# Casting loads for two batches of v, a PSUM bank per pair of heads, and a new order of steps in a linear-attention and FFN kernel

## The chip, the cores and the metric

The kernel runs on one core of a Trainium2 chip. The metric is the device time of one execution in microseconds; the time before is the median of three runs. A core has a matrix engine (TensorE, PE in the profile; its weight loads are PEld), VectorE (DVE), ScalarE (ACT), GpSimd (POOL) and SyncE (SP). They run side by side, each through its own list of instructions in order, and wait for each other by semaphores. GpSimd and SP mostly issue DMA transfers here.

## The reference

Linear attention over 8 batches, 8 heads, 576 positions and head size 64, then a multiplicative feed-forward network over the 4608 rows of 512:

```python
phi(x) = where(x > 0, x, exp(x) - 1) + 1          # = min(max(x, 0) + 1, exp(x))
kv  = sum over s of phi(k)[s, d] * v[s, e];  z = sum over s of phi(k)[s, d]
x   = (phi(q) @ kv) / (phi(q) @ z + 1e-6)
out = ((x @ w1) * (x @ w2)) @ w3 @ w_out
```

Inputs and output are float32.

## The kernel before, in words

Of the 576 positions of a batch, 512 are worked as 4 groups of 128 (`NJ`), the other 64 (`R`) of two batches together as one tile of 128 rows. Eight heads make four pairs (`KC`); a pair fills 128 partitions. The product w3 @ w_out is formed once on the chip (steps `w3t`, `w3c`, `wa`, `wf`, `wc`: w3 is transposed on TensorE, multiplied with w_out, and copied into `wf_sb`), so that each chunk of 512 rows needs only the two products of width 1024, their elementwise product and one more product.

A batch passes through these steps:

- `ld`, `lr`, `lp` load k, q and v; `x` (exp on ACT), `t` (max and add on DVE) and `m` (minimum on DVE) make phi; `xr`, `tr`, `mr` do so for the 64-row rest.
- `v` (L217) casts v to bf16 into `vt`, whose rows have 65 columns: 64 of v and a one, so that a single matmul yields kv and z.
- `kv` (batches 0 and 1) or `kk` (the others) multiply phi(k) with v into PSUM; `kc`, `kh`, `kg` copy the diagonal blocks into `kvb`, which memsets (`const` 4 to 11) have set to zero.
- `qt` and `qc` transpose phi(q) on TensorE for batches 0 and 1, `qd` by a DMA for the others. `na` multiplies with `kvb`; `nd` divides on DVE (add, reciprocal, multiply); `xp` and `xc` (batches 0 to 2) or `xd` (DMA) transpose the result into `xt`.
- Per chunk c and eighth f: step `f` makes both products (8 matmuls of 512 columns, 128 rows of w1 and w2 each), `ac` copies the one to SBUF on ACT, `ab` multiplies them on DVE; `o` makes 128 rows of the output (8 matmuls), `oc` copies them, `st` stores them. Chunk 8 holds the 64-row rests. `ol:7,3` is the last unit, made in two halves of 256 columns, one copied by DVE and stored by SP, one copied and stored by ACT.

PSUM has two pools: `mm_ps`, four tiles of one bank, and `at_ps`, two tiles of two banks, for kv, na and the first part of w3 @ w_out. In SBUF the load pool has 5 buffers, `o_sb` 5, phi of k and q one each, `ab` and `xt` 3.

The order is written out by hand: the string `ORDER` (from L478) lists single steps, and each engine gets its instructions in the order of that list. `v:1,6,2,a` is step `v` of batch 1, two heads from head 6, on ACT; a last letter v, a, g or s names VectorE, ScalarE, GpSimd or SP. `warm` steps are matmuls on zeros whose result nobody reads. `GATES` (L550) adds waits: a load given first may start only when the one given behind `<` has landed. The casting loads of weights (`l3`, `lo`, `lw`) and those of batches 0 and 1 stand in GpSimd's queue, one behind the other; each also waits until the eighth load before it has landed. Loads of later batches, the 64-row rests and DMA transposes stand in SP's queue.

Of the kernel before, what the change touches and what calls it, by code (L numbers as in the profile page):

```python
# [8 lines left out]
F32 = mybir.dt.float32  # L9
# [9 lines left out]
def kernel(  # L19
# [44 lines left out]
    ident = consts.tile([P, P], BF16)  # L64
    zero = consts.tile([P, NCH], BF16)
    vts = [wpool.tile([P, NJ, H, E1], BF16, name=f"vt{i}") for i in range(1)]
    vrz = wpool.tile([P, 2, H, E1], BF16)
    kvb = [wpool.tile([P, KC, 2, E1], BF16, name=f"kvb{i}") for i in range(B)]
# [22 lines left out]


    @step
    def const(i):
        if i == 0:
            nc.vector.memset(zero, 0.0)  # L96
        elif i == 1:
            make_identity(nc, ident)
        elif i == 2:
            for t in vts:  # L100
                nc.vector.memset(t[:, :, :, D:E1], 1.0)
        elif i == 3:
            nc.vector.memset(vrz, 0.0)
            for s in range(2):
                nc.vector.memset(vrz[s * R:(s + 1) * R, s, :, D:E1], 1.0)
        else:
            nc.vector.memset(kvb[i - 4], 0.0)
# [9 lines left out]
    def ld_(n, b, h0, nh, queue):  # L117
# [3 lines left out]
            in_=src[n][b, h0:h0 + nh, 0:NJ * P, :].rearrange("h (p j) d -> p h (j d)", j=NJ))  # L121

# [53 lines left out]
    @step  # L176
    def m(n, b, h0, hp):
        d = got(ph, (n, b), phi_p, [P, KC, NJ, 2, D], BF16, n)
        s = slice((2 * hp - h0) * W, (2 * hp - h0 + 2) * W)
        nc.vector.tensor_tensor(  # L180
            out=d[:, hp].rearrange("p j u d -> p u j d"),
            in0=ts[n, b, h0][:, s].rearrange("p (u j d) -> p u j d", u=2, j=NJ),
            in1=es[n, b, h0][:, s].rearrange("p (u j d) -> p u j d", u=2, j=NJ), op=ALU.min)
# [31 lines left out]
    @step  # L215
    def v_(b, h0, nh, eng):
        copy_of[eng](  # L217
            out=vts[b % len(vts)][:, :, h0:h0 + nh, 0:D],
            in_=raw["v", b].rearrange("p (h j d) -> p j h d", h=H, j=NJ)[:, :, h0:h0 + nh])

    @step
    def vr(b, eng):
        s = b % 2
        r = slice(s * R, (s + 1) * R)
        copy_of[eng](out=vrz[r, s, :, 0:D],
                     in_=raw["vr", b // 2][r].rearrange("p (h d) -> p h d", d=D))
# [3 lines left out]
    def kv(b, hp):  # L230
        o = got(ps, ("kv", b), at_ps, [P, 2, 512], F32, "at", "kvp")
        g, a = divmod(hp, 2)
        kj = ph["k", b]
        kr = ph["kr", b // 2, 2 if b > 1 else b]
        vt = vts[b % len(vts)]
        dst = o[:, g, a * PW:(a + 1) * PW]
        for j in range(NJ):
            nc.tensor.matmul(dst, kj[:, hp, j].rearrange("p u d -> p (u d)"),
                             vt[:, j, 2 * hp:2 * hp + 2, :].rearrange("p h e -> p (h e)"),
                             start=(j == 0), stop=False)  # L240
        nc.tensor.matmul(dst, kr[:, hp * P:(hp + 1) * P],
                         vrz[:, b % 2, 2 * hp:2 * hp + 2, :].rearrange("p h e -> p (h e)"),
                         start=False, stop=True)
# [4 lines left out]
    def kk(b, hp):  # L248
        o = got(ps, ("kk", b), at_ps, [P, 2, 512], F32, "at", "kvp")[:, 0]
        kj, kr, vt = ph["k", b], ph["kr", b // 2, 2], vts[b % len(vts)]  # L250
        for j in range(NJ + 1):
            for u in range(2):
                h = 2 * hp + u
                nc.tensor.matmul(o[u * D:(u + 1) * D, hp * E1:(hp + 1) * E1],  # L254
                                 kj[:, hp, j, u] if j < NJ else kr[:, h * D:(h + 1) * D],
                                 vt[:, j, h] if j < NJ else vrz[:, b % 2, h],
                                 start=(j == 0), stop=(j == NJ))

    @step
    def kg(b, r, eng):  # L260
        rows = slice(r * D, (r + 1) * D)
        copy_of[eng](out=kvb[b][rows, :, r, :], in_=ps["kk", b][rows, 0, 0:KC * E1].rearrange(
# [3 lines left out]
    def kc(b, g0, ng, r, eng):  # L266
        rows = slice(r * D, (r + 1) * D)
        copy_of[eng](  # L268
            out=kvb[b][rows, 2 * g0:2 * (g0 + ng), r, :].rearrange(
                "p (g a) e -> p g a e", a=2),  # L270
            in_=ps["kv", b][rows, g0:g0 + ng, 0:2 * PW].rearrange(
                "p g (a u e) -> p g a u e", a=2, u=2)[:, :, :, r, :])

    @step
    def kh(b, hp, r, eng):
        rows = slice(r * D, (r + 1) * D)
        g, a = divmod(hp, 2)
        c = a * PW + r * E1
        copy_of[eng](out=kvb[b][rows, hp, r, :], in_=ps["kv", b][rows, g, c:c + E1])

    @step
    def qt(b, h, n):
        t = ps["qt", b, h] = mm_ps.tile([P, NCH], F32, tag="mm", name="qtp").bitcast(
            BF16).rearrange("p (i t) -> p i t", t=P)
        for i in range(n):
            for j in range(NJ):
                nc.tensor.transpose(
                    t[:, i * NJ + j, :], ph["q", b][:, h + i, j].rearrange("p u d -> p (u d)"), ident)

    @step  # L290
    def qc(b, h, n, eng):
        d = got(sb, ("qt", b), att, [P, KC, NJ * P], BF16, "qt")
        copy_of[eng](out=d[:, h:h + n, :].rearrange("p i (j t) -> p (i j) t", t=P),
                     in_=ps["qt", b, h][:, 0:n * NJ, :])

    @step
    def qd(b):
        d = got(sb, ("qt", b), att, [P, KC, NJ * P], BF16, "qt")
        nc.sync.dma_start(out=d.rearrange("p c (j t) -> p (c j) t", t=P),
                          in_=ph["q", b].rearrange("p c j u d -> p (c j u d)"), transpose=True)  # L300
# [7 lines left out]
    def na(b, hp):  # L308
        o = ps["na", b, hp] = at_ps.tile([P, 2, 512], F32, tag="at", name="nd")
        for j in range(NJ):  # L310
            nc.tensor.matmul(o[:, j // 2, (j % 2) * 256:(j % 2) * 256 + PW],  # L311
                             sb["qt", b][:, hp, j * P:(j + 1) * P],
                             kvb[b][:, hp].rearrange("p u e -> p (u e)"),
                             start=True, stop=True)

    def divide(o, r, dst):
        nc.vector.tensor_scalar_add(out=r, in0=o[:, :, :, D], scalar1=1e-6)
        nc.vector.reciprocal(out=r, in_=r)  # L318
        nc.vector.tensor_tensor(  # L319
            out=dst, in0=o[:, :, :, 0:D],  # L320
# [269 lines left out]
```

## Time and profile before

| | us |
|---|---|
| runs before, median (lowest to highest) | 251.57 (251.06 to 251.97) |
| the profiled execution's own time | 251.52 |
| its span, first to last instruction | 249.7 |
| busy: TensorE / VectorE / ScalarE / GpSimd | 236.0 / 164.1 / 122.9 / 36.4 |
| first free run of FFN matmuls (`f`) from | 36.36 |
| first output unit (`o:0,0`) from | 55.30 |
| last matmul starts | 246.0 |

The span is what the engines' instructions cover; the time has some 1.8 us more around it. The page gives busy times per engine, the span in 40 slices, the DMA queues, the chain of work that ended last, and groups of instructions with their mean duration and what ended the idle time before them. The timeline, from which single lines are shown below, has: start, duration, engine, line, operation, tiles written and read, count, and in brackets the idle time before it and what ended that.

### The profile page before, as it was taken

To read this page: it belongs to the slowest core of one execution; us is meant where nothing else is said; L and a number is where in the kernel's file an instruction comes from. 1 tells how busy PE (TensorE), PEld (TensorE's weight loads), DVE (VectorE), ACT (ScalarE), POOL (GpSimd) and SP (SyncE) were. 2 spreads that over 40 slices of the span, in tenths; PEclk is the share of its full clock that TensorE was granted. 3 is DMA by queue.
4 is the path that set the end of the run, shared out by engine and by line. 5 is a ranking of instruction groups with operands and counts; after the bars stand their busy time and mean duration, and the time that the engine had idled before them with its cause. 6 is when DMAs were issued, how large, how long until landed. Compare 5 with 4: busy or idle time off the path is not lost.

```text
span 249.7 us, 4327 instructions
## 1 busy us (share of the span) xinstructions
PE 236.0 (95%) x1620; PEld 122.9 (49%) x1636; DVE 164.1 (66%) x364; ACT 122.9 (49%) x190; POOL 36.4 (15%) x59
## 2 busy tenths in 40 slices
PE   6897889979999989999999999999999999999994
PEld 6654844445444555454444454544544444444442
DVE  7518764977868999959649889786775365042320
ACT  3409554776956774665744835153352332323211
POOL 8554720001100210011000032200001100000000
PEclk9999999999999999999999999999999999999999
DMA  6999999999998999999999699975409511210155
GB/s 120 204 265 348 214 198 294 314 248 319 336 240 227 281 294 287 211 248 351 189 265 335 182 248 260 291 175 107 105 12 128 179 22 21 91 38 29 55 144 153
DMA packets 69621, 50.10 MB, mean 201 GB/s; under 512 B 41312, under 2 KB 64096, under 8 KB 69600
## 3 DMA queue, kind: packets, MB, share of 16 engines
q1 hardware_dynamic: 60416, 31.86, 54.1%
q0 software_dynamic: 9040, 17.83, 28.0%
q8 instruction: 13, 0.21, 0.3%
q10 hardware_dynamic: 144, 0.13, 0.2%
q14 instruction: 8, 0.07, 0.1%
HBM read 38.80 MB, written 9.44 MB: 193 GB/s over the span
## 4 chain that ended last, share of the span: by engine, by line
PE 56%; DMA 32%; DVE 4%; issue 3%; ACT 2%; POOL 1%; SPq 0%; ACTq 0%; POOLq 0%; DVEq 0%
PE a_ps L420 17%; PE o_ps L445 17%; PE b_ps L420 17%; DMA v<-in_v_dram 13%; DMA q<-in_q_dram 9%; DMA w_sb<-in_moe_w_dram 4%; DMA wo<-in_moe_w_out_dram 3%; DMA k<-in_k_dram 3%; DVE xn L319 2%; PE nd L311 2%; PE kvp L254 1%; POOL w3b L159 1%; PE ndr L336 1%; PE o_ps L472 1%; ACT vt L217 1%
## 5 line engine op out<-in xcount | busy, mean ns | idle before, releaser
L420 PEld LDWEIGHTS <-w_sb 128*128 128x128 bf16 x576 | 55.6, 98 | 64.6 <-issue 0.6
L439 DVE TENSOR_TENSOR ab<-a_sb,b_ps 128x512 bf16<-128x512 f32 x72 | 49.0, 684 | 43.7 <-PE b_ps L420 40.1
L434 ACT COPY a_sb<-a_ps 128x512 f32<-128x512 f32 x72 | 42.1, 584 | 58.8 <-PE a_ps L420 52.7
L420 PE MATMUL a_ps<-xt,w_sb 128*128 128x512 bf16 x256 | 66.0, 379 | 0.5 <-ACT xt L358 0.5
L420 PE MATMUL b_ps<-xt,w_sb 128*128 128x512 bf16 x256 | 66.0, 379 | 0.0
L445 PE MATMUL o_ps<-wf_sb,ab 128*128 128x512 bf16 x267 | 62.9, 379 | 1.0 <-issue 0.2
L445 PEld LDWEIGHTS <-ab 128*128 128x128 bf16 x280 | 26.4, 98 | 30.3 <-DVE ab L439 1.2
L463 POOL DMA_DIRECT2D out_dram<-o_sb x24 | 14.5, 605 | 148.7 <-ACT o_sb L451 130.9
L451 ACT COPY o_sb<-o_ps 128x512 f32<-128x512 f32 x24 | 14.0, 585 | 34.1 <-PE o_ps L445 31.9
L319 DVE TENSOR_TENSOR xn<-nd,r 128x512 bf16<-128x512 f32 x32 | 22.1, 692 | 1.1
L166 ACT ACTIVATE e<-q 128x1024 bf16<-128x1024 f32 x16 | 16.5, 1056 | 1.8 <-DMA q<-in_q_dram 1.8
L166 ACT ACTIVATE e<-k 128x1024 bf16<-128x1024 f32 x16 | 16.4, 1058 | 0.9 <-DMA k<-in_k_dram 0.8
L451 DVE COPY o_sb<-o_ps 128x512 f32<-128x512 f32 x11 | 7.6, 687 | 8.0 <-PE o_ps L445 8.0
L217 ACT CAST vt<-v 128x1024 bf16<-128x1024 f32 (+1 forms) x11 | 10.2, 933 | 5.4 <-PE kvp L254 2.7
L180 DVE TENSOR_TENSOR k<-t,e 128x512 bf16<-128x512 bf16 x32 | 12.2, 418 | 0.4 <-ACT e L166 0.2
L172 DVE TENSOR_SCALAR t<-q 128x1024 bf16<-128x1024 f32 x16 | 10.9, 688 | 2.1 <-DMA q<-in_q_dram 2.1
L180 DVE TENSOR_TENSOR q<-t,e 128x512 bf16<-128x512 bf16 x32 | 11.9, 420 | 0.2
L311 PE MATMUL nd<-kvb,qt 128*128 128x130 bf16 x128 | 10.9, 220 | 0.9 <-DVE kvb L268 0.4
L172 DVE TENSOR_SCALAR t<-k 128x1024 bf16<-128x1024 f32 x16 | 10.5, 688 | 1.2 <-DMA k<-in_k_dram 1.1
L311 PEld LDWEIGHTS <-qt 128*128 128x128 bf16 x128 | 8.7, 98 | 4.9 <-DVE xn L319 1.0
L113 PE MATMUL warm<-zero 128*128 128x128 bf16 x116 | 9.2, 241 | 1.2 <-DVE zero L96 1.2
L318 DVE RECIPROCAL r<-r 128x8 f32<-128x8 f32 (+1 forms) x40 | 8.1, 202 | 1.4
(76 smaller groups left out, 191.6 us busy)
## 6 DMA issues: line engine op xcount, KB each, us to landing
v<-in_v_dram SPq DMA_DIRECT2D x6, 1024.0 KB, 9.8
k<-in_k_dram SPq DMA_DIRECT2D x6, 1024.0 KB, 8.7
q<-in_q_dram SPq DMA_DIRECT2D x6, 1024.0 KB, 9.2
out_dram<-o_sb POOLq DMA_DIRECT2D x24, 256.0 KB, 6.1
w3b<-in_moe_w_dram POOLq DMA_DIRECT2D x8, 256.0 KB, 8.1
out_dram<-o_sb SPq DMA_DIRECT2D x7, 256.0 KB, 2.3
v<-in_v_dram POOLq DMA_DIRECT2D x3, 512.0 KB, 18.9
out_dram<-o_sb SPq DMA_DIRECT2D x9, 128.0 KB, 2.4
```

The source lines that it names most:

```text
L166: return nc.scalar.activation(out=e[:, 0:nh * W], in_=raw[n, b][:, h0 * W:(h0 + nh) * W], func=AF.Exp)
L172: nc.vector.tensor_scalar(out=d[:, 0:nh * W], in0=raw[n, b][:, h0 * W:(h0 + nh) * W], scalar1=0.0, scalar2=1.0, op0=ALU.max, op1=ALU.add)
L180: nc.vector.tensor_tensor(out=d[:, hp].rearrange("p j u d -> p u j d"), in0=ts[n, b, h0][:, s].rearrange("p (u j d) -> p u j d", u=2, j=NJ ...
L217: copy_of[eng](out=vts[b % len(vts)][:, :, h0:h0 + nh, 0:D], in_=raw["v", b].rearrange("p (h j d) -> p j h d", h=H, j=NJ)[:, :, h0:h0 + nh])
L311: nc.tensor.matmul(o[:, j // 2, (j % 2) * 256:(j % 2) * 256 + PW], sb["qt", b][:, hp, j * P:(j + 1) * P], kvb[b][:, hp].rearrange("p u e - ...
L319: nc.vector.tensor_tensor(out=dst, in0=o[:, :, :, 0:D], in1=r.unsqueeze(3).to_broadcast(list(r.shape) + [D]), op=ALU.mult)
L420: nc.tensor.matmul(o, w[:, kc, f * P:(f + 1) * P], xt_of(c)[:, :, kc, :], start=(kc == 0), stop=(kc == KC - 1))
L434: return copy_of[eng](out=d, in_=ps["a", c, f])
L439: nc.vector.tensor_mul(out=d[:, f, :], in0=sb["a", c, f], in1=ps["b", c, f])
L445: nc.tensor.matmul(d, sb["ab", c][:, f, m * P:(m + 1) * P], wf_sb[:, f, :], start=(f == 0), stop=(f == FC - 1))
L451: return copy_of[eng](out=d, in_=ps["o", c, m])
L463: queue_of[queue].dma_start(out=dst, in_=sb["o", c, m][r])
```

## The change

It has five parts.

1. `v` of batches 0 and 1 is loaded by GpSimd as bf16 (`lv`), without the step `v`; its tile has no ones. In `kv` a 128-column matmul on v is followed by one of two columns on a small tile of ones, with the same weights.
2. `vt`, `vrz` and `kvb` get a new layout: a pair of heads is one row of 130, a one at either end and 128 columns of v between. The cast `v` of later batches takes every second head (`u`) at once.
3. In `kv` each pair has a PSUM bank of its own: the four pairs of a batch take both `at_ps` tiles, where they shared one.
4. phi of k and q is laid out by group, then head; `m` takes the minimum over four heads in one instruction instead of two. `kk` is one step for all pairs of a batch.
5. `ORDER` is new nearly throughout; `st:8,3,s` stands behind `ol:7,3`. Functions `kz`, `nt`, `ln`, `xm` are added that no step of the list calls; a memset for their tile is called.

```diff
+    ones = consts.tile([P, 2], BF16)
+    eps = consts.tile([P, 1], F32)
...
+    kvz = wpool.tile([P, KC, P], BF16)
-    kvb = [wpool.tile([P, KC, 2, E1], BF16, name=f"kvb{i}") for i in range(B)]
+    kvb = [wpool.tile([P, KC, PW], BF16, name=f"kvb{i}") for i in range(B)]
...
+    def of_pairs(t):
+        return t.rearrange("p j (c u) e -> p j c (u e)", u=2)
+
+    def set_ones(t):
+        for c in (0, PW - 1):
+            nc.vector.memset(of_pairs(t)[:, :, :, c:c + 1], 1.0)
...
+        elif i == 12:
+            nc.vector.memset(ones, 1.0)
+            nc.vector.memset(eps, 1e-6)
+            nc.vector.memset(kvz, 0.0)
...
+    def lv(b, h0, nh):
+        if ("vb", b) not in raw:
+            raw["vb", b] = ld.tile([P, H * W], F32, tag="ld", name="vb").bitcast(
+                BF16)[:, 0:H * W].rearrange("p (h j d) -> p h j d", h=H, j=NJ)
+        return nc.gpsimd.dma_start(
+            out=raw["vb", b][:, h0:h0 + nh].rearrange("p h j d -> p h (j d)"),
+            in_=v[b, h0:h0 + nh, 0:NJ * P, :].rearrange("h (p j) d -> p h (j d)", j=NJ))
...
-    def m(n, b, h0, hp):
-        d = got(ph, (n, b), phi_p, [P, KC, NJ, 2, D], BF16, n)
-        s = slice((2 * hp - h0) * W, (2 * hp - h0 + 2) * W)
+    def m(n, b, h0, nh):
+        d = got(ph, (n, b), phi_p, [P, NJ, H, D], BF16, n)
         nc.vector.tensor_tensor(
-            out=d[:, hp].rearrange("p j u d -> p u j d"),
-            in0=ts[n, b, h0][:, s].rearrange("p (u j d) -> p u j d", u=2, j=NJ),
-            in1=es[n, b, h0][:, s].rearrange("p (u j d) -> p u j d", u=2, j=NJ), op=ALU.min)
+            out=d[:, :, h0:h0 + nh].rearrange("p j h d -> p h j d"),
+            in0=ts[n, b, h0][:, 0:nh * W].rearrange("p (h j d) -> p h j d", h=nh, j=NJ),
+            in1=es[n, b, h0][:, 0:nh * W].rearrange("p (h j d) -> p h j d", h=nh, j=NJ), op=ALU.min)
...
     def kv(b, hp):
-        o = got(ps, ("kv", b), at_ps, [P, 2, 512], F32, "at", "kvp")
         g, a = divmod(hp, 2)
-        dst = o[:, g, a * PW:(a + 1) * PW]
+        dst = got(ps, ("kv", b, g), at_ps, [P, 2, 512], F32, "at", "kvp")[:, a, 0:PW]
+        kj, kr, vb = ph["k", b], ph["kr", b // 2, b], raw["vb", b]
         for j in range(NJ):
-            nc.tensor.matmul(dst, kj[:, hp, j].rearrange("p u d -> p (u d)"),
-                             vt[:, j, 2 * hp:2 * hp + 2, :].rearrange("p h e -> p (h e)"),
-                             start=(j == 0), stop=False)
+            k2 = of_pair(kj[:, j], hp)
+            nc.tensor.matmul(dst[:, 1:PW - 1].rearrange("p (u d) -> p u d", u=2), k2,
+                             vb[:, 2 * hp:2 * hp + 2, j], start=(j == 0),
+                             stop=False, skip_group_check=True)
+            nc.tensor.matmul(dst[:, 0:PW:PW - 1], k2, ones, start=False, stop=False, skip_group_check=True)
```

The start and the end of the new list, and its stretch around the loads of batches 1 and 2:

```diff
+    const:0 const:5 lr:k,0,s l3:0 warm:26,0 const:1 warm:18,9 const:3 xr:k,0,0 lr:v,0,s tr:k,0,0 w3t:0
+    l3:1 l3:2 warm:8,1 zr:0,1 w3t:1 w3c:0,a l3:3 lo:0,2 lo:2,2 lo:4,2 lo:6,2 const:4 warm:8,2 l3:4 l3:5
+    const:12 w3t:2 w3c:1,a warm:8,3 ld:k,0,0,4,g w3t:3 w3c:2,v w3c:3,v warm:8,4 mr:k,0,0 wa:0,1
+    ld:k,0,4,4,g wa:1,1 wa:2,1 wa:3,1 wa:4,1 const:6 t:k,0,0,4 ld:q,0,0,4,g w3t:4 vr:0,a ld:q,0,4,4,g
+    wa:5,1 w3c:4,a wa:6,1 const:8 w3t:5 wf:4 x:k,0,0,4 wa:7,1 w3c:5,a lv:0,0,4 wc:4,v m:k,0,0,4 wc:2,a
+    warm:10,10 lv:0,4,2 wc:1,a lv:0,6,2 wc:3,a warm:10,11 warm:10,12 x:k,0,4,4 zr:0,0 t:k,0,4,4 wc:0,v
+    l3:6 warm:10,13 l3:7 lw:0,0,256 lw:1,0,256 x:q,0,4,4 t:q,0,0,4 lw:0,1,256 wf:5 kv:0,0 lw:1,1,256
+    lw:0,1,512 kv:0,1 m:k,0,4,4 t:q,0,4,4 const:2 m:q,0,4,4 x:q,0,0,4 qt:0,2,2 kv:0,3 kh:0,3,1,a
+    m:q,0,0,4 wc:5,a qt:0,0,2 kv:0,2 kh:0,3,0,v qc:0,2,2,v lw:1,1,512 kc:0,0,0,a kc:0,0,1,v w3t:6
+    kh:0,2,0,a na:0,3 qc:0,0,2,a kh:0,2,1,v ld:k,1,0,8,g nd:0,3 w3t:7 na:0,0 w3c:6,a na:0,2 xp:0,3
+    w3c:7,v xc:0,3,a nd:0,0 wf:6 nd:0,2 na:0,1 nd:0,1 xp:0,0 xp:0,2 wf:7 wc:6,v xp:0,1 xc:0,0,a xc:0,1,a
+    ld:q,1,0,8,g xc:0,2,v wc:7,v f:0,2 f:0,1 lr:k,1,s ac:0,2,a ac:0,1,a ab:0,2 lr:v,1,s fk:0,0,0,2
...
+    t:k,1,4,4 m:k,1,4,4 vr:1,v mr:k,0,1 x:q,1,4,4 f:0,5 t:q,1,4,4 kv:1,1 ld:k,2,0,8,s ld:v,2,0,8,s
+    ac:0,5,a ab:0,6 kv:1,0 kv:1,3 m:q,1,4,4 kv:1,2 kc:1,0,0,a kh:1,3,1,v t:q,1,0,4 kh:1,3,0,v qt:1,2,2
+    m:q,1,0,4 qc:1,2,2,a f:0,3 ac:0,3,a ab:0,5 qt:1,0,2 ab:0,3 kh:1,2,0,a kh:1,2,1,a kc:1,0,1,a na:1,3
+    na:1,2 nd:1,3 qc:1,0,2,a o:0,2 nd:1,2 xp:1,3 const:10 x:k,2,4,4 na:1,1 xc:1,3,v na:1,0 o:0,0
...
+    ab:8,5 o:8,1 o:8,2 o:8,0 oc:7,0,a oc:8,1,v o:8,3 oc:8,2,v oc:8,3,v oc:8,0,a st:7,0,s st:8,2,s
+    st:8,1,s st:8,0,s ol:7,3 st:8,3,s
```

The corresponding end of the list before was `... o:8,2 oc:8,0,v st:8,0,s o:7,0 oc:8,2,v st:8,2,s oc:7,0,a st:7,0,s ol:7,3`.

## The prediction

> **What bounds the kernel now.** I read the page first (busy time, the slices), then the sums by stage, then the chain, and last the timeline where the chain changes hands. One matmul can be reported busy while it only drains, so the page's 95% for TensorE is checked by the starts of the matmuls.
>
> ```profile
> PE 236.0 (95%) x1620; PEld 122.9 (49%) x1636; DVE 164.1 (66%) x364; ACT 122.9 (49%) x190; POOL 36.4 (15%) x59
> ...
> DMA  6999999999998999999999699975409511210155
> ```
>
> ```profile
> 0.00:36.00 36.00, 30.05 (x305) 21.40 (x309) 22.08 (x52) 17.38 (x26) 21.84 (x35) 1.00 1.09 226
> 36.00:63.00 27.00, 24.77 (x160) 13.05 (x162) 19.03 (x44) 18.01 (x30) 1.11 (x2) 1.00 1.09 291
> 63.00:125.00 62.00, 60.43 (x466) 30.05 (x470) 52.25 (x120) 41.14 (x63) 5.93 (x10) 1.00 1.10 265
> ...
> 190.00:249.70 59.70, 56.11 (x278) 26.59 (x278) 19.12 (x36) 17.37 (x30) 2.17 (x4) 1.00 0.33 86
> ```
>
> The columns are length, busy time of TensorE, weight load, VectorE, ScalarE and GpSimd, granted clock, DMA share, GB/s. The clock is full throughout. In the trace a 512-column matmul starts 0.216 us after the one before it (four of them make the chain's pieces of 0.86 us), a 128- or 130-column one 0.056 to 0.057 us. Where two starts lie further apart, TensorE lost the difference. Summed: 2.5 us until 11 us (w3 arriving), 1.8 us at 19 us, 2.5 us from 27.7 to 36.4 us, 2.85 us from 50.8 to 63 us (batch 1), 3.7 us from 63 to 190 us, nothing after. Of the 3.7 us about 1 us belongs to the change of tile shape around kk and stays. The tail from the last matmul to the end is 3.6 us. So from 63 us on TensorE is the bound; before that the loads are, with the DMA engines full until about 137 us (22 slices of 6.24 us). The chain says the same:
>
> ```profile
> 1.45 2.25 POOL w3b L159 x4
> 3.70 7.43 DMA wo<-in_moe_w_out_dram
> ...
> 11.41 11.00 DMA q<-in_q_dram
> ...
> 22.69 9.70 DMA w_sb<-in_moe_w_dram
> ...
> 32.68 19.71 DMA v<-in_v_dram
> ...
> 52.41 0.64 ACT vt L217
> ```
>
> One queue of GpSimd loads, beginning at 1.45 us, leads to the second half of v of batch 1 at 52.39 us, its cast, and kv. Any gain must come from this queue, from TensorE's lost time, or from the tail.
>
> **The change, part by part.**
> *First load ahead of the identity.* The GpSimd queue now issues the first w3 load before the two instructions of make_identity, which hold it from 0.74 to 1.31 us. The landings behind it come at a steady pace (w3b 1.25 us apiece), so all move by about 0.6 us. Its cover: the identity is wanted at w3t:0, near 5 us.
>
> *v by casting loads.* Of v of batch 0 one DVE cast of 0.69 us and two ACT casts of 0.63 us go, of batch 1 ACT casts of 1.04 and 0.63 us and a DVE cast of 0.43 us. On the path lies the last one of each: 26.86 us landing to kv at 27.5 us, and in batch 1
>
> ```profile
> 50.70 1.04 ACT L217 CAST vt<-v 128x1024 bf16<-128x1024 f32 x1
> ...
> 51.79 0.39 PE L238 MATMUL kvp<-vt,k 128*128 128x130 bf16 x4 [0.59 <-ACT vt L217]
> ...
> 52.41 0.63 ACT L217 CAST vt<-v 128x512 bf16<-128x512 f32 x1 [0.68 <-DMA v<-in_v_dram]
> ...
> 53.09 0.39 PE L238 MATMUL kvp<-vt,k 128*128 128x130 bf16 x4 [0.58 <-ACT vt L217]
> ```
>
> Here kv waits for a cast twice, 0.6 us each. What the load itself costs: landings of 512 KB of f32 k, q and v follow each other by 1.50 us; the w_sb loads of 256 columns, also 512 KB of source, also cast, also with rows of 1 KB read and 512 B written, by 1.35 us. The Trainium skill, "DMA: Bandwidth & Descriptors", Specifications, gives an HBM limit of about 358 GB/s per core: an estimate of 1.46 us for either kind, so no gain. I follow the nearer rows: 0.3 us less for v of batch 0 and 0.6 us in all at the end of v of batch 1. A bound from the other side: packets of 512 B took 60 ns and of 4 KB 181 ns; one behind another on 16 engines 512 KB take 1.92 against 1.45 us, a loss of 1.9 us over four halves.
>
> *The ones.* With v unpadded, each kv gets four more matmuls of 2 columns, 32 in all. No row shows one. Bounds: kk's 40 matmuls with 64-column weights take 0.98 us, 25 ns apiece; a 128-column matmul with its weights 56 ns. The skill's page "TensorE: Matmul & The Clock Gate", LDWEIGHTS, gives 128/1.2 = 107 ns for the weights, which two columns cannot cover: an estimate of 32 x 107 = 3.4 us. The rows have 128-column weights every 56 ns, so I take 50 ns: 1.6 us, half in batch 0, half in batch 1, part of it in waits for v.
>
> *A bank per pair.* kv of a second pair no longer waits for the copies of its neighbour (0.46 us lost before the matmul at 28.26 us, 0.44 us at 54.21 us). The cost: kv holds both attention buffers, so the first na waits for copies of a whole bank, 0.26 + 0.29 us, but earlier ones.
>
> *Minimum over four heads.* 64 instructions of 0.42 us become 32. Twice as many elements need 0.27 us more (as 0.42 to 0.69 us for casts of 512 and 1024), so 0.69 us each: 26.8 us busy become 22, or 2 us where they run back to back (1.43 us for four now). VectorE is 84% busy from 63 to 125 us and hides it. Against it stand four kvb memsets of 0.49 us moved into this stage and about five xt copies of 0.43 us more on VectorE. I cost the sum at nothing; without cover it would be 2 us.
>
> *The order, front.* wf:7 (1.73 us) goes ahead of the first FFN matmul. Following the new list: w3t:4 now stands before wa:5 and waits for w3 until 16.0 us; wa:7 ends near 21.1 us, its copies (3 x 0.59 us) hold ACT until 23.1 us, then come three exps of 1.06 us to 26.3 us, the minimum to 27.0 us, q's transposes and the last kv to 28.2 us, kvb and qt copies to 28.7 us; then na and four nd of 1.06 us with one w3c of 0.68 us between, to 34.1 us; wf:7, xp, xc: f:0,2 runs freely from 36.0 us. Before, f went on freely at 36.36 us with 0.86 us of it done and wf:7 still to come. Less 0.87 us of work, plus 0.8 us of ones, and 0.36 us earlier: **-0.4 us**.
>
> *Batch 1.* Seven f end at 48.1 us. v's first half lands near 48.8 us, its second near 50.8 us (52.39 less 0.6, 0.6 and some 0.4 us: on the SP queue lp:v,1 moves from ahead of v of batch 2 to behind k of batch 3, and k of batch 2 comes first behind the gate on q of batch 1, so that it starts to share the engines at 47 us). kv waits 0.8 + 0.9 us instead of 2.25 us; f:0,3, kept back, covers the copies, and o between na and xp covers 0.6 us lost there: **-1.1 us**.
>
> *63 to 190 us.* The avoidable 2.7 us are single waits: 0.93 us for nd of batch 2, 0.51 us for v of batch 5, others of 0.1 to 0.3 us. In the new list nd 2,1 has o:1,3 and kk:3 beside it, and v of batch 5 is loaded ahead of q. Other waits will arise; I take half: **-1.2 us**. POOL stores stand in a new sequence, some late (st:0,3, st:2,3), which matters only if five o_sb buffers run out. Later, xdr:3 stands only f:7,3, o:6,3 and o:7,1 (5.2 us) ahead of its reader f:8,2 once f:7,2 is done; ab, ndr:6 and the transpose (0.95 + 1.06 + 2.44 us) take 4.5 us, so it is hidden by 0.7 us.
>
> *Tail.*
>
> ```profile
> 245.94 0.34 SPq L476 DMA_DIRECT2D out_dram<-o_sb  x1
> 246.35 0.37 ACT L474 COPY o_sb<-o_ps 128x256 f32<-128x256 f32 x1 [1.21 <-PE o_ps L472]
> 246.75 0.37 ACTq L476 DMA_DIRECT2D out_dram<-o_sb  x1
> ```
>
> Now the end is ACT's half, landed at 248.62 us. st:8,3, two stores of 64 rows, is put behind SP's half: they issue near 246.3 and 246.85 us and need 2.35 us: 249.2 us, **+0.6 us**.
>
> The sum is -2.1 us on the profiled execution: span 249.7 to 247.6 us, its time 251.52 to 249.4 us. Its own time lies 1.8 us above its span and 0.05 us under the median of the three runs, 251.57 us, so the same sum gives 249.5 us, my forecast.
>
> **The rivals.**
> *Nearly all lost time goes.* Batch 1 as above, all 2.7 us gone: 251.57 - 1.5 - 2.7 + 0.6 = 248.0 us; for it, o and f between attention steps; against it, the DMA engines are full until 137 us and no order makes them faster.
> *Waits move, nothing is gained.* The loads bound both kernels until 63 us, old waits give place to new: -0.4 + 0.6, 251.8 us. For it: DMA share 1.09 and 1.10.
> *Slower: the front slips.* Place: ACT from 21 to 26 us, exps behind three copies that wait for wa:7, then the minimum, now whole halves. Each us by which f:0,2 starts after 36.0 us is a us; from 38.1 us the gain is gone, from 38.9 us it is slower; at 39.2 us, 252.8 us. Against it: each piece has a row.
> *The casting load isn't cheaper.* At packet durations v of batch 0 lands 1.3 us and the end of batch 1's v 2.5 us later than I take: 252.0 us or more. Against it: the w_sb landings.
>
> **How the numbers follow.** My forecast 0.50 (own range 248.6 to 250.9 us), nearly all gone 0.16, waits move 0.14, front slips 0.12, dear casts 0.08. A measurement of this kernel tells about 0.3%, 0.75 us: faster is under 250.8 us, slower over 252.3 us. Faster: 0.45 + 0.16 + 0.05 = 0.66; slower: 0.10 + 0.05 + 0.03 = 0.18; the rest 0.16. Range: low end under "nearly all gone", with the ones at no cost (-0.8 us), 247.2 us; high end 252.4 us leaves out most of the two slow cases.
>
> **What would show it.** First w3 load issued by 0.9 us; v of batch 1 landed by 51 us and no cast before kv; f:0,2 at 36 us; 32 matmuls of 2 columns at about 50 ns; under 1.8 us lost in kv of batch 1; the last landing from SP. Wrong would prove me: f:0,2 after 38 us, lost time over 4 us from 63 to 190 us, or v of batch 1 after 52 us.

## The result, and the profile after

| | before | after |
|---|---|---|
| median of 20 runs (lowest to highest), us | 251.66 (250.89 to 253.23) | 250.23 (249.45 to 251.28) |
| ratio, 95% interval | | 0.9936 (0.992 to 0.9952) |
| the profiled execution's own time / span, us | 251.52 / 249.7 | 250.57 / 248.8 |
| last matmul starts, us | 246.0 | 244.16 |
| from there to the end of the span, us | 3.67 | 4.64 |

Faster by 0.64%, some 1.6 us (1.4 us between the medians), where 2.1 us were forecast, and inside the range. The sum came out within 0.7 us; its terms did not. The first 40 us became slower instead of faster, the stretch from 63 us on gave about twice what I took, and the end cost more.

The page of the changed kernel, busy times and DMA row:

```profile
PE 235.9 (95%) x1668; PEld 123.3 (50%) x1668; DVE 163.2 (66%) x343; ACT 116.5 (47%) x179; POOL 34.2 (14%) x59
...
DMA  6999999999999899999589999896941540131036
```

TensorE has 48 matmuls more in the records and the same busy time. Of the 48, 32 are the ones matmuls; the other 16 are records missing from the trace of before (e_before_vr below, whose matmuls are the same, has 1636). ACT lost 6.4 us, VectorE 0.9 us. The same stages as before the change, in the columns explained there:

```profile
0.00:36.00 36.00, 28.57 (x307) 20.42 (x308) 17.09 (x45) 15.39 (x21) 21.16 (x35) 1.00 1.12 211
36.00:63.00 27.00, 25.87 (x190) 14.01 (x188) 21.19 (x46) 14.49 (x23) 1.12 (x2) 1.00 1.09 279
63.00:125.00 62.00, 62.00 (x450) 31.02 (x449) 50.10 (x104) 40.84 (x63) 4.82 (x9) 1.00 0.99 253
125.00:190.00 65.00, 65.00 (x452) 31.89 (x451) 49.65 (x104) 30.82 (x47) 7.14 (x13) 1.00 0.87 213
```

TensorE is busy without a gap from 63 to 190 us (62.00 of 62.00 and 65.00 of 65.00; before, 60.43 and 64.64). Ahead of 36 us it is less busy than before (28.57 against 30.05). Counted as in the prediction, from the starts of the matmuls, but now with the gaps under 0.1 us, TensorE lost:

| stretch, us | before | after | difference | forecast for that step |
|---|---|---|---|---|
| 0 to 40 | 7.03 | 8.54 | +1.5 (+1.9 with the ones) | -0.4 |
| 40 to 63 | 2.89 | 1.06 | -1.8 (-1.4 with the ones) | -1.1 |
| 63 to 190 | 4.32 | 1.67 | -2.65 | -1.2 |
| last matmul to end | 3.67 | 4.64 | +0.97 | +0.6 |
| sum | | | -1.2 | -2.1 |

The ones matmuls, 0.83 us as measured below, are counted half in each of the first two rows. The span fell by 0.87 us; the 0.3 us left over is the uncertainty of this count. The row from 63 us on is the least sure: by my count of e_before_vr's trace, which lacks none of the output units' matmuls and has the old list from 63 us on, the old list loses some 0.7 to 0.9 us less there than by the trace of before. The gain is then 1.9 to 2.65 us. The profiled executions stand 0.1 us under and 0.3 us over their medians, which makes the 0.95 us between their times the 1.4 us between the medians.

The chain of waits of the changed kernel in its first 40 us (start, length, what):

```profile
1.93 0.23 POOL ident masks.py:197
2.22 0.29 POOL ident masks.py:199
2.51 1.58 POOL w3b L183 x3
4.09 2.77 POOL wo L175 x4
6.86 11.12 DMA w3b<-in_moe_w_dram
...
18.02 0.62 PE w3p L427 x8
...
22.54 0.23 PE wa L444
...
28.17 0.66 DVE q L203
...
28.88 0.62 PE qtp L311 x8
...
38.70 0.59 ACT xt L409
```

The identity now stands between the first and the second w3 load, and the chain runs through it. The fifth w3 load lands at 17.97 us (16.61 before), and everything after hangs on it: w3t:4 at 18.0 us, wa:7, the copies, q's minimum, q's transposes, and the last xt copy, behind which the feed-forward matmuls run from 39.34 us. Ahead of q's minimum it is VectorE and no longer ACT that decides. The timeline there:

```profile
25.47 0.74 POOL L168 DMA_DIRECT2D w_sb<-in_moe_w_dram  x1 [0.73 <-DMA q<-in_q_dram]
25.75 0.95 DVE L196 TENSOR_SCALAR t<-q 128x1024 bf16<-128x1024 f32 x1
25.83 2.01 ACT L190 ACTIVATE e<-q 128x1024 bf16<-128x1024 f32 x2
...
28.13 1.29 DVE L203 TENSOR_TENSOR q<-t,e 128x1024 bf16<-128x1024 bf16 x2
28.88 0.62 PE L311 MATMUL qtp<-ident,q 128*128 128x128 bf16 x8 [0.75 <-DVE q L203]
```

The first of the two exps of q is done by 26.9 us. Its minimum starts at 28.13 us, because VectorE works without a break from 24.0 us on, and q's transposes wait for it.

### The profile page after: what moved, and what is told of

It is laid out like the page before. It is cut to its first block, busy times and chain, and to the rows that moved or that the text cites. A ratio compares the mean times of both kernels' runs of the same rounds, so it can differ in the third digit from the quotient of the medians.

```text
span 248.8 us, 4322 instructions
## 1 busy us (share of the span) xinstructions
PE 235.9 (95%) x1668; PEld 123.3 (50%) x1668; DVE 163.2 (66%) x343; ACT 116.5 (47%) x179; POOL 34.2 (14%) x59
## 4 chain that ended last, share of the span: by engine, by line
PE 84%; DVE 5%; DMA 4%; issue 2%; POOL 2%; ACT 0%; DVEq 0%; ACTq 0%; POOLq 0%
PE o_ps L495 24%; PE a_ps L471 24%; PE b_ps L471 24%; DMA w3b<-in_moe_w_dram 4%; PE nd L334 3%; PE wf_ps L459 2%; PE kvp L282 2%; DVE t L196 1%; PE xtp L404 1%; POOL wo L175 1%; PE qtp L311 1%; PE wa L444 1%; PE ndr L387 1%; PE o_ps L530 1%; POOL w3b L183 1%
## 5 line engine op out<-in xcount | busy, mean ns | idle before, releaser
L471 PEld LDWEIGHTS <-w_sb 128*128 128x128 bf16 x576 | 55.2, 98 | 63.9 <-issue 0.7
L521 POOL DMA_DIRECT2D out_dram<-o_sb x24 | 13.1, 549 | 136.5 <-ACT o_sb L509 81.4
L509 ACT COPY o_sb<-o_ps 128x512 f32<-128x512 f32 x20 | 11.6, 586 | 26.2 <-PE o_ps L495 26.2
L509 DVE COPY o_sb<-o_ps 128x512 f32<-128x512 f32 x15 | 10.2, 687 | 15.5 <-PE o_ps L495 15.4
L196 DVE TENSOR_SCALAR t<-k 128x1024 bf16<-128x1024 f32 x16 | 11.1, 700 | 7.6 <-DMA k<-in_k_dram 7.5
L203 DVE TENSOR_TENSOR k<-t,e 128x1024 bf16<-128x1024 bf16 x16 | 10.9, 685 | 0.8 <-ACT e L190 0.3
L203 DVE TENSOR_TENSOR q<-t,e 128x1024 bf16<-128x1024 bf16 x16 | 10.8, 685 | 0.4
L340 DVE TENSOR_SCALAR r<-nd 128x8 f32<-128x8 f32 x32 | 5.1, 159 | 7.2 <-PE nd L334 7.2
```

Source lines behind the costliest of these rows:

```text
L196: nc.vector.tensor_scalar(out=d[:, 0:nh * W], in0=raw[n, b][:, h0 * W:(h0 + nh) * W], scalar1=0.0, scalar2=1.0, op0=ALU.max, op1=ALU.add)
L203: nc.vector.tensor_tensor(out=d[:, :, h0:h0 + nh].rearrange("p j h d -> p h j d"), in0=ts[n, b, h0][:, 0:nh * W].rearrange("p (h j d) -> p ...
L471: nc.tensor.matmul(o, w[:, kc, f * P:(f + 1) * P], xt_of(c)[:, :, kc, :], start=(kc == 0), stop=(kc == KC - 1))
L509: return copy_of[eng](out=d, in_=ps["o", c, m])
L521: queue_of[queue].dma_start(out=dst, in_=sb["o", c, m][r])
```

## The experiments

The kernels of the experiments ran in three groups on three chips, each group beside the kernel before: e_ident, e_tail, e_oldorder and e_oldfront; e_stores, e_onebank and e_f32v; the other four. Interval and ratio are against the kernel before of the same group.

| kernel | median, us | ratio | 95% interval |
|---|---|---|---|
| changed kernel | 250.23 | 0.9936 | 0.992 to 0.9952 |
| e_ident | 249.57 | 0.9908 | 0.988 to 0.9937 |
| e_tail | 250.49 | 0.994 | 0.9921 to 0.996 |
| e_oldorder | 251.84 | 0.9982 | 0.9951 to 1.0012 |
| e_oldfront | 249.37 | 0.9917 | 0.9886 to 0.9948 |
| e_stores | 249.39 | 0.99 | 0.9869 to 0.993 |
| e_onebank | 249.84 | 0.9926 | 0.9898 to 0.9954 |
| e_f32v | 252.97 | 1.0034 | 1.0015 to 1.0053 |
| e_oldorder_vr | 250.67 | 0.9971 | 0.9952 to 0.9989 |
| e_before_vr | 251.98 | 1.0003 | 0.9986 to 1.002 |
| e_twohead | 250.01 | 0.9945 | 0.9922 to 0.9967 |
| e_best | 248.88 | 0.9887 | 0.9869 to 0.9905 |

### The front: the identity between two loads

```diff
-    const:0 const:5 lr:k,0,s l3:0 warm:26,0 const:1 warm:18,9 ...
+    const:0 const:5 lr:k,0,s const:1 l3:0 warm:26,0 warm:18,9 ...
```

> The changed kernel with one step moved: make_identity stands again ahead of the first w3 load, as it did before the change. Theory A (the identity between the first and the second w3 load starves the queue: in the trace after, the second load is issued at 2.46 us instead of 2.12 us and lands at 8.79 instead of 7.41 us, and everything behind it on the queue, up to q of batch 0 at 25.19 instead of 23.91 us, is 1.3 us later): the second w3 load lands near 7.4 us, q of batch 0 near 23.9 us, the first feed-forward matmuls run freely about 1 us earlier, and the time falls by 0.5 to 1.2 us against the changed kernel, to 249.0 to 249.7 us. Theory B (one of the 16 DMA engines fell behind by chance or because of the v remainder load; the identity has nothing to do with it): landings stay where they are, time 250.0 to 250.5 us.

Measured: 249.57 us, ratio 0.9908; beside it on the same chip e_tail, which has the front of the changed kernel, 250.49 us and 0.994. The second w3 load is issued at 2.12 us again and lands at 7.68 us, q of batch 0 at 24.29 us. Landings differ from one execution to the next, so I compare all traces. In those with the identity between the loads (the changed kernel, e_tail) the second half of q of batch 0 lands at 25.19 and 24.89 us; in the eleven others with the new code or the old at 24.17 to 24.72 us, and in the profiled execution of before at 23.92 us. That is 0.6 us on average for the identity in the landings: theory A holds there, at half its size. The medians agree: e_ident is 0.9 us under e_tail, of which 0.35 us is the longer end of e_tail (4.96 against 4.61 us in the traces), and 0.7 us under the changed kernel, though there the intervals overlap. The +1.5 us in the table above is more than that, partly because the profiled execution of before has the earliest landings of all and that of after the latest.

How the 0.6 us reach TensorE the traces show less well. The first feed-forward matmul starts at 38.50 us in the changed kernel and at 37.61 us in e_ident, but in e_tail, with the identity between the loads, at 37.56 us. The difference is made on VectorE between 23 and 27 us. Two `t` steps there take 0.96 and 0.95 us in the changed kernel, and 0.92 to 0.99 us in e_ident and the three others with this front and the identity first, e_stores, e_onebank and e_twohead; alone in e_tail they take 0.69 and 0.68 us, like the other `t` steps of these traces. They run beside GpSimd's issues of two w_sb loads, and in e_tail it is these that take longer, 1.22 and 0.88 us instead of 0.75 and 0.74 us. So one of the two engines seems to wait for the other, and which one is worth some 0.5 us here; no run tests it. The profiled execution of e_tail took 249.93 us, 0.56 us less than its median, so its trace is the lucky one.

e_oldfront puts the whole front back, up to the first feed-forward unit, and lets the new order follow:

```diff
+    (the list of before up to:) ... fk:0,0,2,1 fk:0,0,3,1 ac:0,0,a ab:0,0
+    (then the new list, without what is done:) ... wf:7 wc:7,v f:0,2 f:0,1 lr:k,1,s ...
```

> The changed kernel's code and order, but everything up to the first feed-forward unit of batch 0 in the order of the kernel before (what is still to be done then follows in the new order). Theory A (the new order of the front costs 2.2 us, of which 0.4 us are the ones matmuls, while the new order behind it gains by itself): feed-forward matmuls run freely near 37 to 38 us with wf:7 done, and the time is 248.2 to 249.2 us. Theory B (the gain from 63 us on hangs on loads and copies that the new front puts elsewhere): the front is faster, but the lost time from 40 to 125 us rises, and the time is 249.8 us or more.

Measured: 249.37 us, 0.2 us over the upper end of theory A, and not to be told from e_ident. The lost time behind the front did not rise, so theory B is out. By its trace kv of batch 1 ends 0.4 us ahead of e_ident. So of the new front only the place of the identity costs what can be measured; for the rest of the new front, wf:7 ahead of the first feed-forward matmul included, neither a gain nor a loss shows.

### Code or order

```diff
-    ORDER = """ (the new list) """
+    ORDER = """ (the list of before, lv for ld:v, one m for two, one kk for four, const:12 at the start) """
```

> The changed kernel's code (casting v loads, ones matmuls, a bank per pair, minimum over four heads) run in the order of the kernel before, each step in its old place. Theory A (the gain is the order's work: TensorE loses 2.7 us less from 63 us on, and the code's parts bring what they bring only in kv of batches 0 and 1): time 250.3 to 251.3 us, with 2.5 us or more of TensorE's time still lost between 63 and 190 us. Theory B (the code's parts bring the gain, through a VectorE that is 5 us less busy, and the order gives little or costs something in the front): 248.5 to 250.0 us. Theory C (the parts cost, the order pays for them): over 251.6 us.

Measured: 251.84 us, not to be told from before and by the median in theory C's range. The stages from 63 us on of its trace:

```profile
63.00:125.00 62.00, 60.83 (x468) 30.19 (x470) 50.89 (x102) 39.97 (x61) 4.95 (x9) 1.00 1.11 264
125.00:190.00 65.00, 64.60 (x415) 31.79 (x418) 51.51 (x109) 29.06 (x44) 5.17 (x9) 1.00 0.79 197
```

TensorE is busy 60.83 and 64.60 us, as before the change (60.43 and 64.64), and loses 4.2 us from 63 to 190 us where the new order loses 1.7 us. So the gain from 63 us on is the order's; a part of the code in it does not show. That much of theory A is shown. From 40 to 63 us this trace loses only 0.9 us, as little as the changed kernel (1.1 us): the gain of batch 1 is the code's. But that execution took 250.09 us, and nine of the fourteen took 251.2 to 253.0 us. A second trace of the same kernel asks why.

> The same kernel as e_oldorder (the new code in the old order, whose times lay between 249.96 and 253.0 us), for one more trace. Theory A (the old order leaves waits for single loads, so that loads which land somewhat later in one execution than in another move the end): if its time is over 251.5 us, the lost time of TensorE is 1.5 us or more above the first trace's 11.2 us, and the places are waits for v, k or q. Theory B (the spread is the front's, w3 and wo landing up to 1 us apart, as in any order): the surplus lies before 36 us.

It took 252.85 us. The timeline of this second trace, three lines, and of the first trace, one line:

```profile
48.03 0.43 DVE L248 CAST vrz<-v32r 64x512 bf16<-64x512 f32 x1 [5.69 <-DMA v32r<-in_v_dram]
48.49 0.69 DVE L490 TENSOR_TENSOR ab<-a_sb,b_ps 128x512 bf16<-128x512 f32 x1
...
49.23 0.59 PE L471 MATMUL b_ps<-xt,w_sb 128*128 128x512 bf16 x2 [1.64 <-DVE ab L490]
```

```profile
43.58 0.43 DVE L248 CAST vrz<-v32r 64x512 bf16<-64x512 f32 x1 [1.45 <-DMA v32r<-in_v_dram]
```

Step vr:1,v casts the 64 remaining rows of v. The old order has it on VectorE ahead of the feed-forward products; its 128 KB load, on the SP queue beside the GpSimd queue, landed at 43.6 us in one execution and at 48.0 us in the other. In the other VectorE stood still for 5.69 us, the product `ab` behind the cast was late, no buffer was free for `b_ps`, and TensorE waited 1.8 us and later 0.7 us. Theory A's account of that execution holds. In the changed kernel the same load landed at 47.40 us and harmed nobody, because there vr:1,v stands behind k's minimum. Whether this explains the spread as a whole, the next kernel asks: the old order with that step alone moved.

```diff
-    ab:0,3 f:0,5 wc:7,a vr:1,v ac:0,5,a ...
+    ab:0,3 f:0,5 wc:7,a ac:0,5,a ... m:k,1,4,4 vr:1,v ...
```

> e_oldorder (the new code in the old order) with one step moved: vr:1,v, the cast of v's remainder rows of batches 0 and 1 for batch 1 on DVE, from ahead of the feed-forward products and k of batch 1 to behind k's minimum, where the new order has it. Theory A (in the second trace of the old order this cast waited on DVE for its 128 KB load until 48.0 us, and two feed-forward units behind it lost 1.8 and 0.7 us, while in the first trace the load was there at 43.6 us; the new order is faster in the median mainly because this step is out of the way): the median falls from 251.8 to 249.9 to 250.5 us, and the times lie within about 1.5 us of each other instead of 3 us. Theory B (the spread has other causes as well, such as the first loads): median 250.8 us or more, spread 2.5 us or more.

Measured: 250.67 us, between the two theories. Executions over 251.2 us became rarer (5 of 22 instead of 9 of 14), the lowest stayed where they were (249.81 against 249.96 us), and four still took 252.3 to 252.8 us. So the cast's place is very likely one cause of the spread; another stays open. The ratio, 0.9971, can't be told from that of e_oldorder, but its interval lies under 1: with this step out of the way the code gains some 0.7 us in the old order, and theory C of e_oldorder is out.

And the same move in the kernel before:

```diff
-    ab:0,3 f:0,5 wc:7,a vr:1,v ac:0,5,a ...
+    ab:0,3 f:0,5 wc:7,a ac:0,5,a ... m:k,1,4,3 vr:1,v ...
```

> The kernel before the change with the same single step moved: vr:1,v behind k's last minimum of batch 1. Theory A (the wait of this cast for its load is in most executions of the kernel before, though the profiled one shows it with little harm): the median falls by 0.4 to 1.2 us, to 250.6 to 251.4 us beside 251.8 us, and the executions above 252.3 us go. Theory B (in the kernel before kv of batch 1 waits for v and its casts anyway until 52.4 us, so that DVE has the time): no change beyond 0.3 us.

Measured: 251.98 us, ratio 1.0003, nothing. Its trace shows why: kv of batch 1 still waits 0.42, 0.84 and 0.44 us for v and its casts and for the copies, until 55.2 us. There VectorE had the time, as theory B says. The step is worth moving only once the casts are gone.

### The parts of the code, undone one by one

All three have the identity first and are compared with e_ident. v loaded as f32 and cast after landing:

```diff
-            raw["vb", b] = ld.tile([P, H * W], F32, tag="ld", name="vb").bitcast(BF16)...
+            raw["v", b] = ld.tile([P, H * W], F32, tag="ld", name="v")...
+            raw["vb", b] = vbx
...
+    def vc(b, h0, nh, eng):
+        copy_of[eng](out=vbx[:, h0:h0 + nh], in_=raw["v", b][:, h0:h0 + nh])
```

> The changed kernel with make_identity first (e_ident, 249.57 us), but v of batches 0 and 1 loaded as f32 and cast afterwards, 4 + 2 + 2 heads, on DVE and ACT as before the change, into a bf16 tile laid out as the casting load leaves it; kv and the ones matmuls stay. Theory A (the casting load lands 0.3 to 0.4 us per 512 KB earlier, and the cast of 0.6 us is off the path ahead of kv): v of batch 1 lands 1 us or more later, kv of batch 1 waits again for casts, 1.2 to 2.4 us more of TensorE's time is lost up to 63 us, and the time is 250.6 to 252.0 us. Theory B (TensorE's other waits cover it, as q and k decide when kv and na can run): 249.4 to 250.2 us.

Measured: 252.97 us, 3.4 us over e_ident and slower than before the change; theory A, and beyond its range. v of batch 1 lands at 50.13 and 51.61 us, where in e_ident it landed at 48.74 and 50.09 us. The wait that this makes, in the timeline:

```profile
53.37 0.22 PE L270 MATMUL kvp<-vbx,k 128*128 128x128 bf16 x1 [1.54 <-ACT vbx L151]
```

and the stages around it, with TensorE's granted clock in the third column from the end:

```profile
51.00:53.40 2.40, 0.86 (x5) 0.33 (x4) 2.34 (x5) 2.40 (x4) 0.00 (x0) 1.00 1.02 355
...
54.40:56.00 1.60, 1.60 (x23) 1.60 (x23) 0.27 (x2) 0.19 (x1) 0.00 (x0) 0.52 1.09 357
56.00:58.00 2.00, 2.00 (x10) 1.00 (x9) 1.96 (x5) 1.01 (x1) 0.00 (x0) 0.53 1.10 349
58.00:60.00 2.00, 1.95 (x22) 1.40 (x22) 1.00 (x4) 1.54 (x5) 0.00 (x0) 1.00 1.11 337
```

Behind the gap of 1.9 us between two matmuls the clock is at 0.52 and 0.53 in stretches of 1.6 and 2.0 us, which is half clock for some 3.4 us and costs some 1.7 us more than the wait itself. The last matmul starts 3.86 us later than in e_ident: 1.35 us come from the front (feed-forward from 38.96 instead of 37.61 us), where v of batch 0 is cast again and, in this execution, q lands 0.4 us later; about 1.7 us come from the clock, the rest from the waits in batch 1. The list of executions agrees: those with a mean clock of 1.0 took 251.4 to 252.4 us, those with 0.993 252.4 to 253.5 us, those with 0.989 253.8 to 254.0 us.

One attention buffer for kv again, two pairs to a bank:

```diff
-        dst = got(ps, ("kv", b, g), at_ps, ...)[:, a, 0:PW]
+        dst = got(ps, ("kv", b), at_ps, ...)[:, g, a * PW:(a + 1) * PW]
```

> The changed kernel with make_identity first (e_ident, 249.57 us), but with kv of all pairs in one attention buffer again, two pairs to a bank, and the copies of kv reading it there. Theory A (the bank per pair removes waits of kv for the copies of the neighbour's pair, of 0.46 us in batch 0 and 0.44 us in batch 1): a wait of 0.2 to 0.5 us comes back before kv of the fourth pair in one or both batches, time 249.9 to 250.5 us. Theory B (in the new order transposes and feed-forward matmuls stand between the copies and the next kv, so the bank does not matter): no change, 249.3 to 249.9 us, and the second buffer is free earlier.

Measured: 249.84 us, ratio 0.9926, its interval overlapping that of e_ident: theory B. No wait before the kv of a fourth pair came back, as transposes or feed-forward matmuls stand ahead of it in the new order. In the front the waits at na are 0.70, 0.79 and 0.28 us instead of 1.03 and 0.71 us, the same sum. The bank per pair is worth nothing in this order that these runs could show.

The minimum in two instructions of two heads:

```diff
+        for i in range(0, nh, 2):
+            s = slice(i * W, (i + 2) * W)
...
-            in0=ts[n, b, h0][:, 0:nh * W]...
+            in0=ts[n, b, h0][:, s]...
```

> The changed kernel with make_identity first (e_ident, 249.57 us), and the minimum of each half again made in two instructions of two heads: 64 of 0.42 us in place of 32 of 0.68 us on DVE, 5 us of DVE time more, in the same places of the order. Theory A (DVE is hidden; I costed this part at nothing): within 0.3 us of e_ident, 249.3 to 249.9 us. Theory B (DVE is near its limit from 63 to 125 us and its copies and products feed TensorE): 0.5 to 2 us slower, 250.1 to 251.6 us, with waits of TensorE for DVE between 63 and 125 us or in the front ahead of q's transposes.

Measured: 250.01 us, 0.1 us over the upper end of theory A and 0.4 us over e_ident, with intervals that overlap. The stage where VectorE has most to do:

```profile
63.00:125.00 62.00, 62.00 (x445) 30.74 (x443) 50.98 (x118) 41.26 (x64) 4.84 (x9) 1.00 0.99 251
```

TensorE is busy 62.00 of 62.00 us, as in the changed kernel, with VectorE at 50.98 instead of 50.10 us. In the front q's transposes wait 0.75 and 0.28 us instead of 0.93 us. So from 63 us on the trace shows theory A, the minimum over four heads hidden; a few tenths, ahead of q's transposes for example, can be neither shown nor excluded.

### The end

The timeline of the changed kernel's end:

```profile
244.10 0.34 SPq L534 DMA_DIRECT2D out_dram<-o_sb  x1
244.49 1.11 SPq L521 DMA_DIRECT2D out_dram<-o_sb  x2
...
244.91 0.37 ACTq L534 DMA_DIRECT2D out_dram<-o_sb  x1
```

SP's half is followed by the two stores of st:8,3, the second of them issued at 245.0 us and landed at 247.75 us, last of all, as forecast. But ACT's half, issued at 244.91 us, landed at 247.44 us, 2.5 us later; before the change it took 1.87 us. The first kernel moves st:8,3 back:

```diff
-    ... st:8,0,s ol:7,3 st:8,3,s
+    ... st:8,0,s st:8,3,s ol:7,3
```

> The changed kernel with the last store of the main rows, st:8,3, put back ahead of the halved unit. Theory A (the store behind SP's half is what ends last, at 247.75 us, against ACT's half at 247.44 us): the end moves to ACT's half, 0.3 to 0.5 us earlier, time 249.7 to 249.9 us, and the tail after the last matmul falls from 4.6 to about 4.2 us. Theory B (the SP queue is full at the end and SP's half then ends last instead): no change, 250.1 to 250.3 us.

Measured: 250.49 us, ratio 0.994: no gain. Now SP's half is issued at 244.17 us behind eight stores and lands 2.94 us later at 247.12 us, ACT's half 2.95 us after its issue at 246.91 us; from the last matmul to the end it is 4.96 us. That is theory B: to take the one late store away from the end is no cure. Next, each store right behind its copy (on e_ident):

```diff
-    o:8,1 o:8,2 o:8,0 oc:7,0,a oc:8,1,v o:8,3 oc:8,2,v oc:8,3,v oc:8,0,a st:7,0,s st:8,2,s st:8,1,s st:8,0,s ol:7,3 st:8,3,s
+    o:8,1 oc:7,0,a st:7,0,s o:8,2 oc:8,1,v st:8,1,s o:8,0 oc:8,2,a st:8,2,s o:8,3 oc:8,0,v st:8,0,s oc:8,3,a st:8,3,s ol:7,3
```

> The changed kernel with make_identity first (as in e_ident, 249.57 us there) and with the last stores on SP in the order in which their units finish: st:7,0, st:8,1, st:8,2, st:8,0, st:8,3, each behind its copy, copies in turn on DVE and ACT, the halved unit last. Theory A (in the new order SP waits with st:7,0 and st:8,2 ahead of st:8,1, so that nine stores stand one behind another from 240 us on and land 2.6 to 2.95 us after their issue instead of 1.9 us): the tail after the last matmul falls from 4.6 to about 3.7 us, and the time to 248.4 to 249.0 us. Theory B (the tail is longer for another cause, such as two stores of 64 rows where one is made for other units): tail 4.3 us or more, time 249.3 to 249.9 us.

Measured: 249.39 us, tail 4.20 us, the halves 2.41 us after their issue: between the theories, and the time not to be told from e_ident. What still differed from the end before the change was the unit just ahead of the halves: two stores of 64 rows instead of one of 128. The last kernel, with e_oldfront's front, changes that:

```diff
-    f:8,5 ... o:7,0 ... ab:8,5 o:8,1 o:8,2 o:8,0 ... o:8,3 ... ol:7,3 st:8,3,s
+    f:8,5 o:7,2 ... ab:8,5 st:7,2,s o:8,1 o:8,2 ... o:8,0 ... o:8,3 ... o:7,0 ... st:7,0,s ol:7,3
```

> The changed kernel with the front in the old order (as in e_oldfront, 249.37 us) and with a new end: o:7,2 in place of o:7,0 beside the last product, then the four units of the remainder rows, o:7,0 and the halved unit, with each store right behind its copy. The last store ahead of the halved unit is then one of 128 rows, as before the change. Theory A (in e_stores the tail stayed at 4.2 us because two stores of 64 rows, which land 2.4 to 2.6 us after their issue, stand just ahead of the halves): the tail falls to 3.7 us and the time to 248.4 to 249.1 us. Theory B (the tail is not set by the form of the stores ahead): 4.1 us or more, 249.2 us or more.

Measured: 248.88 us, ratio 0.9887, its interval below that of the changed kernel. From e_oldfront, whose front it has, the time can't be told; the end can, where e_oldfront has 4.72 us. The timeline of its end:

```profile
243.51 0.34 SPq L534 DMA_DIRECT2D out_dram<-o_sb  x1
...
244.32 0.38 ACTq L534 DMA_DIRECT2D out_dram<-o_sb  x1
```

The halves land at 245.41 and 246.20 us, 1.90 and 1.88 us after their issue, and the tail is 3.67 us, as before the change: theory A. Whether a store of 64 rows holds up those behind it by its form, or only because two follow each other more closely than one, these runs don't fully separate. The form alone isn't it: SP's half in the changed kernel, in e_ident and in e_oldfront also stands behind a store of 64 rows, but is issued 0.95 to 0.96 us after it, and lands 1.98 to 2.01 us after its own issue. With 0.68 us between (e_stores) it is 2.41 us, with 0.69 us (e_tail) 2.94 us; in e_best 0.77 us lie between it and a store of 128 rows. In e_stores the two halves also follow each other by 0.38 us, in e_best by 0.81 us.

## Why the prediction was right or wrong

*First load ahead of the identity (forecast: all loads 0.6 us earlier).* Wrong in sign. The step left out that the identity, moved off the first load, now holds up the second: the first was issued 0.19 us earlier (1.26 against 1.45 us), the second 0.34 us later (2.46 against 2.12 us), and the loads behind it some 0.6 us later. Moving it back is worth some 0.6 us (e_ident against e_tail, less the end).

*Front (-0.4 us, f:0,2 free at 36.0 us).* Wrong: 39.34 us, past the 38 us that I had named as refuting. The list of dates began with w3 for w3t:4 at 16.0 us, which landed at 17.97 us; ACT's copies then ended at 25.0 instead of 23.1 us, the exps at 27.8 instead of 26.3 us. For what follows the list named the wrong engine: not ACT's exps but VectorE held q's minimum, to 28.13 us, with `t` steps and a memset that the list doesn't have. The other 1.4 us of the 3.3 us went between 27 and 32 us, where I had counted one minimum of q and one copy of its transposes, and two of each stand in turn with kv. This is the rival "the front slips", about at its size but not in its place: it named ACT between 21 and 26 us, where nothing more was lost; 2.0 us came ahead of it, with w3, and the rest behind it. By the medians of e_ident and e_oldfront 0.7 to 0.9 us can be had back, though the intervals overlap that of the changed kernel; some of what the two traces differ by was early and late landings.

*Casting loads (0.15 us less per 512 KB).* Right in kind, too small: the two halves of v took 2.51 us in batch 0 and 2.40 us in batch 1 of the changed kernel from q's landing on, as f32 2.94 us (batch 0 before, batch 1 of e_f32v). That is 0.2 to 0.27 us per half. The Trainium skill's limit ("DMA: Bandwidth & Descriptors", Specifications) would have made it nothing; f32 loads keep to the 1.46 us estimated from it, casting loads, at 1.20 to 1.25 us, do not. The part was worth more than I gave it, 1.8 us or more with full clock in e_f32v, where the casts, the later landings behind the f32 loads and the waits that follow come together.

*Ones (1.6 us).* Right in kind, half the size. Between the starts of a matmul on v and the next in kv:

```profile
27.20 0.22 PE L264 MATMUL kvp<-vb,k 128*128 128x128 bf16 x1
...
27.25 0.17 PE L267 MATMUL kvp<-ones,k 128*128 128x2 bf16 x1
...
27.28 0.22 PE L264 MATMUL kvp<-vb,k 128*128 128x128 bf16 x1
```

0.08 us with the two columns, 0.056 us without: 26 ns each, 0.83 us for 32. I had taken 50 ns; the lower bound that I gave, kk's 25 ns, was the price. The page "TensorE: Matmul & The Clock Gate" has both figures: its time for loading weights, 107 ns, is near what one load takes in the trace (95 to 98 ns) but doesn't set the distance between starts, and its floor for a small matmul ("Wait — 56ns, not 53.3ns?"), about 25 ns from start to start, agrees. I had cited the one and passed over the other.

*Bank per pair (removes 0.46 and 0.44 us).* The waits are gone, but e_onebank shows that the order took them away, not the banks. *Minimum over four heads (nothing).* Right from 63 us on: 0.685 us each, and hidden; in the front VectorE was not idle, and what the step is worth there stays open.

*Batch 1 (-1.1 us).* Right in size, -1.4 us, but not as described. v landed at 49.47 and 50.77 us (forecast 48.8 and 50.8 us), and kv was to wait for it 0.8 and 0.9 us from 48.1 us on. TensorE came to kv only at 51.20 us, about as much later as the front had slipped; v was there, kv lost 0.27 us ahead of the 64-row rest and q's transposes 0.70 us. So part of the front's loss stands where the wait for v would have been. e_oldorder has the smaller loss (0.9 us) in the old order too: it is the code's gain, provided that VectorE isn't held by vr:1,v.

*63 to 190 us (-1.2 us).* Right in kind, mis-sized: -1.9 to -2.65 us. I called half of the avoidable 2.7 us removable; all of it was, by the order alone (e_oldorder keeps the old losses). This is the rival "nearly all lost time goes", for this stretch.

*Tail (+0.6 us).* The sign and the last landing, from SP, were right, the size and most of the cause not: +0.97 us. The late store ends 0.3 us behind ACT's half (247.75 against 247.44 us); the other 0.65 us is ACT's half itself, which lands 2.52 instead of 1.87 us after its issue, with the stores of 64 rows issued 0.43 us before and 0.08 us after it. The forecast took that landing as given.

*The clock ("full throughout").* Not at the start: until 4.1 us the warm matmuls of the kernel before start 0.107 us apart, behind that 0.056 us. The rows show 1.00 there all the same. It is so in the changed kernel too and doesn't touch the comparison.

That the forecast came near is luck: two rivals of opposite sign both came true, one in the front and one behind it, and by my own sign (f:0,2 after 38 us) the case I held likeliest did not happen. A range made of such cases held.

## What to carry to other kernels

When a step is moved away from one instruction of a queue, look at which one it now stands in front of: the identity cost some 0.6 us between the first and the second load. A cast that waits for a small load belongs behind the work that others wait for; in one execution it is harmless and in the next it costs 2 us, which a single trace doesn't show. What is issued just ahead of the last stores counts as much as the last stores themselves.

## What I had not expected of the hardware

A gap of 1.9 us between two matmuls was followed by half clock for some 3.4 us (e_f32v, 0.52 and 0.53), and 15 of its 22 executions have the mean clock of this one, 0.993, or a lower one. The length of the gap alone doesn't decide: gaps of 2.8 us (changed kernel, at 6 us) and 2.0 us (second trace of e_oldorder, at 47 us) left the clock at 1.00 in the windows behind them. The other thing is two `t` steps of VectorE, which took 0.92 to 0.99 us beside GpSimd's issues of loads in five traces with the new front, and 0.69 us in a sixth, in which the issues took longer. And a load of 128 KB on the SP queue, beside full GpSimd loads, landed 12.3 to 15.5 us after its issue, between 43.6 and 48.0 us, in kernels that issued it within 1.4 us of each other.
